# A fused causal convolution and SwiGLU block on one core: cast and transpose of x by transfers instead of by engines

## Chip, cores and metric

The kernel runs on one core of one Trainium2 chip. The metric is device time in microseconds (us), the median of several runs.

## The reference, cut to what matters

```python
# x: 8 x 4096 x 192, weight: 8 heads x 7 taps; w_gate, w_val: 192 x 1536; w_out: 1536 x 192
w = softmax(weight, axis=-1)                       # per head, 24 channels each
x_pad = concatenate([zeros(B, 6, D), x], axis=1)   # six zero rows ahead of each sequence
y[b, s, c] = sum_k w[head(c), k] * x_pad[b, s + k, c]      # seven taps
y = y.reshape(32768, 192)
g = y @ w_gate
out = (g * sigmoid(g) * (y @ w_val)) @ w_out       # float32
```

## The kernel before, in words

The 32768 tokens are cut into 64 blocks of 512 (`TB`), and the blocks go in 32 pairs; a sequence is 4 pairs (`ppb`). The 192 channels of one block are 128 and 64 (`P` and `DB`), so the convolution of a pair is done in three groups of 128 partitions with tokens along the free axis: `A0` and `A1`, the first 128 channels of either block, and `B`, the last 64 of both.

The main loop counts chunks (`at`): a block has 12 (`NCH`), one for 128 of the 1536 hidden columns, a pair has 24. In a chunk `Block.first` multiplies the convolved tokens by the gate and value weights. With 192 = 3 x 64 it uses the two halves of TensorE's rows side by side: gate from partitions 0 to 63 (L344), value from 64 to 127 (L345), three of each. For this each group's result `xc` also exists with its halves swapped, `xs`, which two transfers on SP's queue make (`swap`, L318 and L319). `gate` has ACT write `silu` (L349) and VectorE multiply it by `val` into `h` (L351). `second` multiplies the `h` of the block before by the output weights (L356), four pairs of matmuls a chunk; every sixth chunk ACT copies two finished sub-blocks out (`evacuate`, L394) and SP stores them (`store`, L386). In PSUM, `gate` has two banks, `val` three, `acc` two, and the transposed input `xt` one.

While a pair is multiplied, the next one is convolved. SP fetches x of a pair as float32 with the 128 tokens before it (`emit_fetch`, L73), two pairs ahead; POOL casts it to fp16 in three instructions (`emit_cast`, L210 to L212; L203 to L206 for the first pair, where ACT helps). TensorE transposes each group by matmuls with an identity, 64 x 64 at a time, low and high halves mixed with the matmuls of `second` (`turns`, L265; nine a group), with waits on SP to keep the order inside a bank (`mark`, L222). Of the seven taps ACT copies the transposed group to SBUF (`copy`, L283) and makes three products from that copy (`start_d`, L287, and two `act_tap`, L291); VectorE adds two taps into `aD`, reading the transposed group in PSUM (`dve_tap`, L295); POOL makes two products (`pool_tap`, L302) and adds up (L308, and `join`, L312).

Every engine works off its instructions in the order in which the program issues them. That order is written out by hand: `PLAN["start"]` gives the chunk of the pair in which each group's transposes stand (`first` for pair 1), the other entries how many chunks later each step of the group is issued.

The opening (pair 0) is separate: the transposes of pair 0 are 128 wide (`turn`, L249 and L251), the swapped halves of its first block come from TensorE (L443), group `B` is convolved by TensorE (`sumB`, L424) with matrices that VectorE makes (`diag`, L410), and POOL issues the casting transfers of the weights (L121, L451).

Of the kernel before, what the change touches and what calls it, by code (L numbers as in the profile page):

```python
# [13 lines left out]
    start={"B": 0, "A0": 7, "A1": 15},  # L14
    first={"B": 4, "A0": 10, "A1": 18},
    aP1=(3, 5), taps1=(2, 3), pool1=5, nact1=2, npool1=2,
    copy=1, aD=2, aP=(4, 6), taps=(2, 4), pool=6, fetch=6, fetch1=10, cast=11,
    swap={"B": 13, "A0": 12, "A1": 13}, swap1={"B": 11, "A0": 11, "A1": 11},
    nact=2, npool=2, gate=2, val=3,
# [4 lines left out]
def kernel(  # L24
# [40 lines left out]
    tpool = ctx.enter_context(tc.tile_pool(name="xts", bufs=1, space=bass.MemoryType.PSUM))  # L65
# [3 lines left out]
    def emit_fetch(p, later_than=None):  # L69
        x_sb = xpool.tile([P, 1 + 2 * SUBS, D], fp32, tag="x_sb", name="x_sb", bufs=2)  # L70
        t0 = p * 2 * TB
        lo = 0 if p % ppb else 1
        ins = nc.sync.dma_start(  # L73
            out=x_sb[:, lo:, :],
            in_=x_flat[t0 - P * (1 - lo) : t0 + 2 * TB, :].rearrange("(s p) d -> p s d", p=P),
        )
# [15 lines left out]
    x_sbs = {0: xpool.tile([P, 1 + 2 * SUBS, D], fp32, tag="x_sb", name="x_sb", bufs=2)}  # L92
    halves = [
        nc.sync.dma_start(
            out=x_sbs[0][:, 1 + b * SUBS :, :][:, 0:SUBS, :],
# [4 lines left out]


# [13 lines left out]

    if n_pairs > 1:
        x_sbs[1] = emit_fetch(1, halves[1])

    def load_w(lo, hi, which):
# [24 lines left out]
        for n, shape, dt in (  # L144
            ("xt_act", [P, DB + TB], fp16),
            ("wn_ps", [P, 2, K], fp32),
# [4 lines left out]
            ("idle", [P, TB], fp32),  # L151
        )
# [8 lines left out]
    own = const_pool.tile([H, D + DB], fp32, tag="own", name="own")  # L161
    nc.gpsimd.memset(own, 1.0)
    for m, at in ((own[:, 0:D], 0), (own[:, D:], P)):
        n = m.shape[1]
        nc.gpsimd.affine_select(
            out=m, in_=m, pattern=[[1, n]],
            compare_op=ALU.is_ge, fill=0.0, base=at, channel_multiplier=-grp,
        )
        nc.gpsimd.affine_select(
            out=m, in_=m, pattern=[[-1, n]],  # L170
            compare_op=ALU.is_ge, fill=0.0, base=grp - 1 - at, channel_multiplier=grp,
        )
# [12 lines left out]
    wn = const_pool.tile([P, 2, K], fp32, tag="wn", name="wn")  # L185
    for g in range(2):
# [3 lines left out]
    wsm = {"A": wn[:, 0, :], "B": wn[:, 1, :]}  # L190

    x16s = {}

    def emit_cast(p, first=False):
        x_sb = x_sbs.pop(p)
        xa = xpool.tile([P, 1 + 2 * SUBS, P], fp16, tag="xa", name="xa", bufs=2)
        xb = xpool.tile([P, 1 + SUBS, 2, DB], fp16, tag="xb", name="xb", bufs=2)
        lo = 0 if p % ppb else 1
        if lo:
            nc.gpsimd.memset(xb[:, 0, 0, :], 0.0)  # L200
            nc.gpsimd.memset(xa[:, 0, :], 0.0)
        if first:
            nc.gpsimd.tensor_copy(xa[:, lo : SUBS + 1, :], x_sb[:, lo : SUBS + 1, 0:P])  # L203
            nc.scalar.copy(xb[:, lo:, 0, :], x_sb[:, lo : SUBS + 1, P:D])
            nc.scalar.copy(xb[:, :, 1, :], x_sb[:, SUBS:, P:D])
            nc.gpsimd.tensor_copy(xa[:, SUBS + 1 :, :], x_sb[:, SUBS + 1 :, 0:P])  # L206
            for b in range(2):
                load_w(C1, 2 * C1, b)
        else:
            nc.gpsimd.tensor_copy(xb[:, lo:, 0, :], x_sb[:, lo : SUBS + 1, P:D])  # L210
            nc.gpsimd.tensor_copy(xb[:, :, 1, :], x_sb[:, SUBS:, P:D])
            nc.gpsimd.tensor_copy(xa[:, lo:, :], x_sb[:, lo:, 0:P])  # L212
        x16s[p] = xa, xb


# [10 lines left out]
    def mix(long, short):  # L226

        n = max(len(long), 1)
        for i in range(n):
            if long:  # L230
                long[i]()
            for t in short[i * len(short) // n : (i + 1) * len(short) // n]:
                t()

    class Group:


        def __init__(self, p, g, pool=cpool):
            self.p, self.g, self.w, self.pool = p, g, wsm[g[0]], pool
            self.parts = []  # L240

        def rows(self, s):
            xa, xb = x16s[self.p]
            if self.g == "B":
                return xb[:, s, :, :].rearrange("p b c -> p (b c)")
            return xa[:, s + SUBS * (self.g == "A1"), :]
# [9 lines left out]

        def turns(self):


            self.xt = tpool.tile([P, DB + TB], fp16, tag="xt", name="xt")  # L260
            ends = []

            def one(s, r):
                at = s * P - DB + r
                ins = nc.tensor.transpose(  # L265
                    self.xt[:, at : at + DB], self.rows(s)[r : r + DB, :], ident[r : r + DB, r : r + DB]
                )
                if (s, r) == (0, DB):
                    sync_after(ins, ends[0])
                if (s, r) == (SUBS, 0):  # L270
                    ends.append(mark(ins))

            low = [lambda s=s: one(s, 0) for s in range(1, SUBS + 1)]
            high = [lambda s=s: one(s, DB) for s in range(SUBS + 1)]
            return low, high
# [46 lines left out]
    class Block:  # L322
# [11 lines left out]
        def first(self, j):  # L334
# [72 lines left out]
    nc.vector.tensor_copy(part[0], wsm["B"])  # L407
    nc.vector.tensor_tensor(part[1], wsm["B"], part[0], op=ALU.subtract)
# [31 lines left out]
    for g, ps, copy in (("A0", idle, nc.vector.tensor_copy), ("B", early["swB"], nc.scalar.copy)):  # L440
# [25 lines left out]
    def plan(x):  # L466
        na, npl = PLAN["nact" + x], PLAN["npool" + x]
        ks = [1 + i for i in range(6)]
        acts, dves, pools = ks[:na], ks[na : 6 - npl], ks[6 - npl :]

        def pool_work(g):
            own, g.parts = g.parts, []
            for k in pools:
                g.pool_tap(k)
            for a in own:
                g.parts.append(a)
                g.add()
            g.join()

        steps = [(PLAN["copy"], Group.copy), (PLAN["aD"], lambda g: g.start_d(False))]  # L480
        for k, o in zip(acts, PLAN["aP" + x]):
            steps.append((o, lambda g, k=k: g.act_tap(k, False)))
        for k, o in zip(dves, PLAN["taps" + x]):
            steps.append((o, lambda g, k=k: g.dve_tap(k)))
        return steps + [(PLAN["pool" + x], pool_work)]

    plans = {"": plan(""), "1": plan("1")}

    before = None
    owed, high = [], []  # L490
    todo = {}
    at = 0
    for p in range(n_pairs):
        for bi in range(2):
            block = Block(2 * p + bi)
            for j in range(NCH):
                if at % 24 == PLAN["fetch" if p else "fetch1"] and p + 2 < n_pairs:
                    x_sbs[p + 2] = emit_fetch(p + 2)
# [83 lines left out]
```

## Time and profile before

| what | value |
|---|---|
| median of 3 runs | 789.12 us (788.87 to 789.64) |
| profiled execution: span from first to last instruction | 787.6 us |
| granted TensorE clock, mean | 1.000 |
| from the start to the first `gate` matmul | 15.4 us |
| one pair of the middle, 24 chunks | 23.9 us |
| DMA, mean rate | 88 GB/s |

The profiled execution is one more run, and its time is known by its span; the runs' median is 1.5 us above it. Lines like L345 are lines of the kernel before. PE is TensorE's matmuls, PEld its weight loads, DVE VectorE, ACT ScalarE, POOL GpSimd, SP the engine that issues most transfers (SPq: its queue). Rows of groups give busy time and the mean duration of one instruction; matmuls overlap, so that their rows add up to more than the time they take.

### The profile page before, as it was taken

The numbers are of one execution on the slowest core, as the hardware profiler recorded it, in microseconds if no ns is written. First come the engines' busy times: TensorE is split into PE (matmuls) and PEld (weight loads), VectorE is DVE, ScalarE is ACT, GpSimd is POOL, SyncE is SP. The second block draws the span as 40 slices with busy tenths as digits, with TensorE's granted clock in tenths as the row PEclk, the third lists the DMA queues.
The fourth block names the chain that finished last, engine by engine and source line by source line (L and its number), as shares of the span: only waits on it lengthen the run. The fifth ranks groups of instructions, "written<-read, shape, count | busy, mean of one in ns | idle before, by whom it ended". The sixth has DMA issues, their size and how long they took to land.

```text
span 787.6 us, 29354 instructions
## 1 busy us (share of the span) xinstructions
PE 778.4 (99%) x11635; PEld 695.8 (88%) x11635; DVE 638.3 (81%) x980; ACT 701.0 (89%) x1286; POOL 670.0 (85%) x689
## 2 busy tenths in 40 slices
PE   7999999999999999999999999999999999999998
PEld 3789999999999999999999999999999999999997
DVE  7888888878888888888888888788888888888874
ACT  6999999999899989899999999998999898999974
POOL 7899898888899888898888998888998888988840
PEclk9999999999999999999999999999999999999999
DMA  9333313333223333223333133332233332233111
GB/s 192 80 100 93 91 53 100 97 86 104 78 69 100 92 92 90 69 85 92 103 95 90 55 94 97 91 103 80 62 101 98 90 89 67 85 95 104 48 46 52
DMA packets 89178, 69.07 MB, mean 88 GB/s; under 512 B 7248, under 2 KB 88656, under 8 KB 89040
## 3 DMA queue, kind: packets, MB, share of 16 engines
q1 hardware_dynamic: 86656, 65.82, 29.5%
q0 software_dynamic: 2384, 1.38, 1.2%
q8 instruction: 91, 1.49, 0.8%
q14 instruction: 47, 0.39, 0.2%
HBM read 31.06 MB, written 25.17 MB: 71 GB/s over the span
## 4 chain that ended last, share of the span: by engine, by line
PE 96%; DMA 2%; POOL 1%; SPq 0%; ACT 0%; issue 0%; DVE 0%
PE val L345 35%; PE gate L344 31%; PE acc L356 27%; PE xt L265 2%; DMA x_sb<-in_x_dram 2%; ACT silu L349 0%; SPq L113 0%; POOL xcA L312 0%; POOL t L308 0%; POOL xa L212 0%; PE gate L356 0%; PE val L356 0%; ACT t L291 0%; DVE h L351 0%; SPq L319 0%
## 5 line engine op out<-in xcount | busy, mean ns | idle before, releaser
L351 DVE TENSOR_TENSOR h<-silu,val 128x512 f16<-128x512 f16 x768 | 513.5, 684 | 138.4 <-ACT silu L349 69.2
L349 ACT ACTIVATE silu<-gate 128x512 f16<-128x512 f32 x768 | 449.2, 595 | 70.6 <-PE gate L344 57.6
L356 PE MATMUL acc<-wo_sb,h 64*128 64x192 f16 x6096 | 421.6, 243 | 0.3 <-DVE h L351 0.3
L308 POOL TENSOR_TENSOR t<-t,t 128x512 f32<-128x512 f32 x281 | 357.2, 1271 | 62.6 <-ACT t L291 47.1
L356 PEld LDWEIGHTS <-h 64*128 64x128 f16 x6144 | 372.5, 94 | 25.7 <-DVE h L351 0.5
L344 PE MATMUL gate<-xcA,w_sb 64*128 64x512 f16 x768 | 288.7, 376 | 1.5 <-ACT silu L349 0.8
L345 PE MATMUL val<-xcA,w_sb 64*128 64x512 f16 x768 | 288.8, 376 | 0.4 <-DVE h L351 0.4
L345 PE MATMUL val<-xsA,w_sb 64*128 64x512 f16 x768 | 288.8, 376 | 0.0
L344 PE MATMUL gate<-xsA,w_sb 64*128 64x512 f16 x768 | 288.7, 376 | 0.0
L344 PEld LDWEIGHTS <-w_sb 64*128 64x128 f16 x2304 | 209.2, 94 | 28.1 <-issue 1.1
L345 PEld LDWEIGHTS <-w_sb 64*128 64x128 f16 x2304 | 208.1, 94 | 9.5 <-issue 2.4
L295 DVE SCALAR_TENSOR_TENSOR aD<-xt,wn,aD 128x512 f32<-128x512 f16 x194 | 145.0, 748 | 0.4 <-PE xt L251 0.2
L344 PE MATMUL gate<-xsB,w_sb 64*128 64x512 f16 x384 | 144.4, 376 | 0.0
L345 PE MATMUL val<-xcB,w_sb 64*128 64x512 f16 x384 | 144.4, 376 | 0.0
L345 PE MATMUL val<-xsB,w_sb 64*128 64x512 f16 x384 | 144.4, 376 | 0.0
L344 PE MATMUL gate<-xcB,w_sb 64*128 64x512 f16 x384 | 144.3, 376 | 0.0
L302 POOL TENSOR_SCALAR t<-xcin,wn 128x512 f32<-128x512 f16 x186 | 127.0, 697 | 13.2 <-ACT xcin L283 13.1
L291 ACT ACTIVATE t<-xcin,wn 128x512 f32<-128x512 f16 x188 | 134.2, 714 | 0.0
L312 POOL TENSOR_TENSOR xcA<-t,aD 128x512 f16<-128x512 f32 x63 | 80.0, 1269 | 4.9
L287 ACT ACTIVATE aD<-xcin,wn 128x512 f32<-128x512 f16 x94 | 67.0, 713 | 0.0
L394 ACT COPY o<-acc 128x384 f32<-128x384 f32 x126 | 60.6, 481 | 3.0 <-PE acc L356 0.6
L283 ACT COPY xcin<-xt 128x518 f16<-128x518 f16 x94 | 55.0, 585 | 0.9 <-PE xt L265 0.7
(78 smaller groups left out, 256.7 us busy)
## 6 DMA issues: line engine op xcount, KB each, us to landing
out_dram<-o SPq DMA_DIRECT2D x128, 192.0 KB, 2.0
x_sb<-in_x_dram SPq DMA_DIRECT2D x24, 864.0 KB, 5.2
xsA<-xcA SPq DMA_DIRECT2D x126, 64.0 KB, 2.0
x_sb<-in_x_dram SPq DMA_DIRECT2D x7, 768.0 KB, 4.9
xsB<-xcB SPq DMA_DIRECT2D x62, 64.0 KB, 2.0
x_sb<-in_x_dram SPq DMA_DIRECT2D x2, 384.0 KB, 3.9
wo_sb<-in_moe_w_out_dram POOLq DMA_DIRECT2D x1, 576.0 KB, 7.5
w_st<-in_moe_w_gate_dram SPq DMA_DIRECT2D x1, 384.0 KB, 4.6
```

What stands on the lines that cost most here:

```text
L287: nc.scalar.mul(self.aD, *self.tap(0, psum, xt))
L291: nc.scalar.mul(self.parts[-1], *self.tap(k, psum, xt))
L295: nc.vector.scalar_tensor_tensor(out=self.aD, in0=v, scalar=s, in1=self.aD, op0=ALU.mult, op1=ALU.add)
L302: nc.gpsimd.tensor_scalar(self.parts[-1], v, scalar1=s, scalar2=1.0, op0=ALU.mult, op1=ALU.mult)
L308: nc.gpsimd.tensor_tensor(self.parts[0], self.parts[0], t, op=ALU.add)
L312: (eng or nc.gpsimd).tensor_tensor(xc, self.parts[0], self.aD, op=ALU.add)
L344: nc.tensor.matmul(g, w[0:DB, ca, f], a[0:DB, :], start=(i == 0), stop=(i == 2))
L345: nc.tensor.matmul(v, w[DB:P, cb, f], b[DB:P, :], start=(i == 0), stop=(i == 2))
L349: nc.scalar.activation(s, self.g.pop(j), AF.Silu)
L351: nc.vector.tensor_tensor(h, s, self.v.pop(j), op=ALU.mult)
L356: ins = nc.tensor.matmul(acc, self.h[j][r, ts(s, P)], wo_r[r, j, :], start=first and j == 0, stop=not first and j == NCH - 1, skip_group_c ...
L394: nc.scalar.copy(self.o[:, 2 * half : 2 * half + 2, :], self.acc[:, :, 0:D])
```

## The change

From pair 1 on, a casting transfer issued by POOL (`emit_cast`) copies x from DRAM to a DRAM buffer in fp16, 528 rows of 384: the 16 tokens before and the 512 of a block, with both blocks of the pair side by side. One transposing transfer issued by SP (`emit_turn`) brings it to SBUF as `xt`, 128 x 3 x 528. The 384 columns make three groups of 128: block 0's channels 0 to 127; its last 64 with block 1's first 64; block 1's last 128. `Group` works on `xt` in SBUF in place of `xcin` and PSUM: the transposing matmuls (`turns`), ACT's copy, POOL's casts and the order waits go, and VectorE's taps read SBUF (`dve_tap` with `psum=False`, in the opening for the last group of pair 0 as well). At the head of a sequence POOL zeroes 16 columns (`emit_blank`). The order is given anew, in chunks before the pair's first chunk: cast at -54, transposing transfer at -40, groups from -27, -19 and -11; for pair 1, whose cast and transfer are issued in the opening, groups from chunks 3, 9 and 16. `gate` gets the PSUM bank that becomes free, and the pools of the main loop take over the opening's banks tile by tile (`reuse_waits`).

```diff
 PLAN = dict(
-    start={"B": 0, "A0": 7, "A1": 15},
-    first={"B": 4, "A0": 10, "A1": 18},
-    aP1=(3, 5), taps1=(2, 3), pool1=5, nact1=2, npool1=2,
-    copy=1, aD=2, aP=(4, 6), taps=(2, 4), pool=6, fetch=6, fetch1=10, cast=11,
-    swap={"B": 13, "A0": 12, "A1": 13}, swap1={"B": 11, "A0": 11, "A1": 11},
-    nact=2, npool=2, gate=2, val=3,
+    start=(-27, -19, -11),
+    first=(3, 9, 16),
+    aD=0, aP=(2, 4), taps=(1, 3), pool=4, swap=11,
+    cast=-54, turn=-40,
+    nact=2, npool=2, gate=3, val=3,
 )
...
-    tpool = ctx.enter_context(tc.tile_pool(name="xts", bufs=1, space=bass.MemoryType.PSUM))
+    dpool = ctx.enter_context(tc.tile_pool(name="x16d", bufs=3, space=bass.MemoryType.DRAM))
...
-    def emit_fetch(p, later_than=None):
...
+    HIST = 16
+    ROWS = HIST + TB
+    drams, xts = {}, {}
+
+    def emit_cast(q):
+        t0 = q * 2 * TB - HIST
+        d = dpool.tile([ROWS, 2 * D], fp16, tag="x16d", name="x16d")
+        src = bass.AP(
+            tensor=x_flat.tensor,
+            offset=x_flat[t0 : t0 + 1, :].offset,
+            ap=[[D, ROWS], [TB * D, 2], [1, D]],
+        )
+        nc.gpsimd.dma_start(out=d[:, :].rearrange("r (b c) -> r b c", b=2), in_=src)
+        drams[q] = d
+
+    def emit_turn(q):
+        xt = xpool.tile([P, 3, ROWS], fp16, tag="xt", name="xt", bufs=3)
+        nc.sync.dma_start(out=xt[:, :, :], in_=drams.pop(q)[:, :], transpose=True)
+        xts[q] = xt
+
+    def emit_blank(q):
+        nc.gpsimd.memset(xts[q][:, 0, 0:HIST], 0.0)
+        nc.gpsimd.memset(xts[q][0:DB, 1, 0:HIST], 0.0)
...
-    x_sbs = {0: xpool.tile([P, 1 + 2 * SUBS, D], fp32, tag="x_sb", name="x_sb", bufs=2)}
+    x_sb = xpool.tile([P, 2 * SUBS, D], fp32, tag="x_sb", name="x_sb", bufs=1)
...
-        x_sbs[1] = emit_fetch(1, halves[1])
...
-    def emit_cast(p, first=False):
...
+    x16 = xpool.tile([P, 1 + SUBS, 2, D], fp16, tag="x16", name="x16", bufs=1)
+    nc.gpsimd.memset(x16[:, 0, 0, :], 0.0)
+    nc.gpsimd.tensor_copy(x16[:, 1:, 0, 0:P], x_sb[:, 0:SUBS, 0:P])
+    nc.scalar.copy(x16[:, 1:, 0, P:D], x_sb[:, 0:SUBS, P:D])
+    nc.scalar.copy(x16[:, :, 1, 0:DB], x_sb[:, SUBS - 1 :, 0:DB])
+    nc.gpsimd.tensor_copy(x16[:, :, 1, DB:D], x_sb[:, SUBS - 1 :, DB:D])
+    for b in range(2):
+        load_w(C1, 2 * C1, b)
...
-            self.p, self.g, self.w, self.pool = p, g, wsm[g[0]], pool
+            self.p, self.g, self.w, self.pool = p, g, wn[:, g, :], pool
+            if p:
+                self.xc_in = xts[p][:, g, HIST - pad :]
             self.parts = []
...
-        def turns(self):
...
-            return low, high
...
-        def dve_tap(self, k):
-            v, s = self.tap(k)
+        def dve_tap(self, k, psum=False):
+            v, s = self.tap(k, psum)
...
-            A, B = f"A{self.bi}", "B"
-            xA, sA, xB, sB = xcs[self.p, A], xcs[self.p, A, "S"], xcs[self.p, B], xcs[self.p, B, "S"]
-            lo = ((xA, 0), (sA, 1), (sB if self.bi else xB, 2))
-            hi = ((xA, 1), (sA, 0), (xB if self.bi else sB, 2))
+            a, b = (1, 2) if self.bi else (0, 1)
+            xA, sA, xB, sB = xcs[self.p, a], xcs[self.p, a, "S"], xcs[self.p, b], xcs[self.p, b, "S"]
+            if self.bi:
+                lo = ((sA, 0), (xB, 1), (sB, 2))
+                hi = ((xA, 0), (sB, 1), (xB, 2))
+            else:
+                lo = ((xA, 0), (sA, 1), (xB, 2))
+                hi = ((xA, 1), (sA, 0), (sB, 2))
...
-            A1.turn(tpool.tile([P, DB + TB], fp16, tag="xt", name="xt"))
+            A1.turn(early["xtC"])
...
     if n_pairs > 1:
         emit_cast(1)
+    if n_pairs > 2:
+        emit_cast(2)
     for k in (2, 3, 4, 5):
         A1.dve_tap(k)
     A1.add()
     A1.join()
+    if n_pairs > 1:
+        emit_turn(1)
     A1.swap()
     opening.close()
...
-    gpool = ctx.enter_context(tc.tile_pool(name="gates", bufs=PLAN["gate"], space=bass.MemoryType.PSUM))
-    vpool = ctx.enter_context(tc.tile_pool(name="vals", bufs=PLAN["val"], space=bass.MemoryType.PSUM))
-    apool = ctx.enter_context(tc.tile_pool(name="acc", bufs=1, space=bass.MemoryType.PSUM))
-
-
-
-    def plan(x):
...
-    plans = {"": plan(""), "1": plan("1")}
+    gpool = ctx.enter_context(tc.tile_pool(name="gates", bufs=PLAN["gate"], reuse_waits="tile", space=bass.MemoryType.PSUM))
+    vpool = ctx.enter_context(tc.tile_pool(name="vals", bufs=PLAN["val"], reuse_waits="tile", space=bass.MemoryType.PSUM))
+    apool = ctx.enter_context(tc.tile_pool(name="acc", bufs=1, reuse_waits="tile", space=bass.MemoryType.PSUM))
...
+    todo = {}
+
+    def at_chunk(c, f):
+        todo.setdefault(c, []).append(f)
+
+    ks = list(range(1, K))
+    na, npl = PLAN["nact"], PLAN["npool"]
+    acts, dves, pools = ks[:na], ks[na : len(ks) - npl], ks[len(ks) - npl :]
+
+    def pool_work(g):
...
+    def plan_group(q, g, c):
+        def begin():
+            group = Group(q, g)
+            group.start_d(False)
+            for k, o in zip(acts, PLAN["aP"]):
+                at_chunk(c + o, lambda k=k: group.act_tap(k, False))
+            for k, o in zip(dves, PLAN["taps"]):
+                at_chunk(c + o, lambda k=k: group.dve_tap(k))
+            at_chunk(c + PLAN["pool"], lambda: pool_work(group))
+            at_chunk(c + PLAN["swap"], group.swap)
+
+        at_chunk(c + PLAN["aD"], begin)
+
+    for q in range(1, n_pairs):
+        base = 2 * NCH * q
+        if q > 2:
+            at_chunk(base + PLAN["cast"], lambda q=q: emit_cast(q))
+        if q > 1:
+            at_chunk(base + PLAN["turn"], lambda q=q: emit_turn(q))
+        if q % ppb == 0:
+            at_chunk(base + PLAN["start"][0] - 2, lambda q=q: emit_blank(q))
+        for g in range(3):
+            plan_group(q, g, base + PLAN["start"][g] if q > 1 else PLAN["first"][g])
...
-                if at % 24 == PLAN["fetch" if p else "fetch1"] and p + 2 < n_pairs:
-                    x_sbs[p + 2] = emit_fetch(p + 2)
                 end = before is not None and j % 6 == 5
                 los, his = before.second(4) if before is not None else ([], [])
                 if not end:
                     block.first(j)
-                if high and high[0] <= at:
-                    mix(owed, high[1])
-                    owed, high = [], []
-                if p + 1 < n_pairs:
...
                 for lo, hi in zip(los, his):
                     lo()
                     hi()
-                if before is not None and j % 6 == 5:
+                if end:
                     before.evacuate(j // 6)
-                if end:
                     block.first(j)
                 block.gate(j)
-                if before is not None and j % 6 == 5:
+                if end:
                     before.store(j // 6)
-                for f, gr in todo.pop(at, ()):
-                    f(gr)
+                for f in todo.pop(at, ()):
+                    f()
...
```

More of the change, by code (lines that the diff above doesn't have):

```diff
@@ L64 @@
     opool = ctx.enter_context(tc.tile_pool(name="out", bufs=2))
-    tpool = ctx.enter_context(tc.tile_pool(name="xts", bufs=1, space=bass.MemoryType.PSUM))
+    dpool = ctx.enter_context(tc.tile_pool(name="x16d", bufs=3, space=bass.MemoryType.DRAM))
     ctx.enter_context(tc.manual_schedule())
-    def emit_fetch(p, later_than=None):
[L70 to L75, printed above, removed]
-        )
-        if later_than is not None:
-            sync_after(ins, later_than, "the first pair goes first")
-        return x_sb
+    HIST = 16
[8 more added lines that the diff above has]
+            ap=[[D, ROWS], [TB * D, 2], [1, D]],
+        )
+        nc.gpsimd.dma_start(out=d[:, :].rearrange("r (b c) -> r b c", b=2), in_=src)
[7 more added lines that the diff above has]
+        nc.gpsimd.memset(xts[q][0:DB, 1, 0:HIST], 0.0)
     def sync_after(ins, earlier, why="one bank, two halves of the array"):
@@ L91 @@
     nc.sync.dma_start(out=taps, in_=weight)
-    x_sbs = {0: xpool.tile([P, 1 + 2 * SUBS, D], fp32, tag="x_sb", name="x_sb", bufs=2)}
+    x_sb = xpool.tile([P, 2 * SUBS, D], fp32, tag="x_sb", name="x_sb", bufs=1)
     halves = [
         nc.sync.dma_start(
-            out=x_sbs[0][:, 1 + b * SUBS :, :][:, 0:SUBS, :],
+            out=x_sb[:, b * SUBS : (b + 1) * SUBS, :],
             in_=x_flat[b * TB : (b + 1) * TB, :].rearrange("(s p) d -> p s d", p=P),
@@ L114 @@
         )
-    if n_pairs > 1:
-        x_sbs[1] = emit_fetch(1, halves[1])
     def load_w(lo, hi, which):
@@ L145 @@
             ("xt_act", [P, DB + TB], fp16),
-            ("wn_ps", [P, 2, K], fp32),
+            ("wn_ps", [P, 3, K], fp32),
             ("xtB", [P, DB + TB], fp16),
@@ L151 @@
             ("idle", [P, TB], fp32),
+            ("xtC", [P, DB + TB], fp16),
         )
@@ L158, in warm @@
             nc.tensor.matmul(idle, ident, zeros, start=True, stop=True)
-    own = const_pool.tile([H, D + DB], fp32, tag="own", name="own")
+    own = const_pool.tile([H, 2 * D], fp32, tag="own", name="own")
     nc.gpsimd.memset(own, 1.0)
-    for m, at in ((own[:, 0:D], 0), (own[:, D:], P)):
-        n = m.shape[1]
+    for m in (own[:, 0:D], own[:, D:]):
         nc.gpsimd.affine_select(
-            out=m, in_=m, pattern=[[1, n]],
-            compare_op=ALU.is_ge, fill=0.0, base=at, channel_multiplier=-grp,
+            out=m, in_=m, pattern=[[1, D]],
+            compare_op=ALU.is_ge, fill=0.0, base=0, channel_multiplier=-grp,
         )
         nc.gpsimd.affine_select(
-            out=m, in_=m, pattern=[[-1, n]],
-            compare_op=ALU.is_ge, fill=0.0, base=grp - 1 - at, channel_multiplier=grp,
+            out=m, in_=m, pattern=[[-1, D]],
+            compare_op=ALU.is_ge, fill=0.0, base=grp - 1, channel_multiplier=grp,
         )
@@ L184 @@
     wn_ps = early["wn_ps"]
-    wn = const_pool.tile([P, 2, K], fp32, tag="wn", name="wn")
-    for g in range(2):
+    wn = const_pool.tile([P, 3, K], fp32, tag="wn", name="wn")
+    for g in range(3):
         nc.tensor.matmul(wn_ps[:, g, :], own[:, ts(g, P)], soft, start=True, stop=True)
@@ L189 @@
     nc.vector.tensor_copy(wn, wn_ps)
-    wsm = {"A": wn[:, 0, :], "B": wn[:, 1, :]}
-    x16s = {}
-    def emit_cast(p, first=False):
[L195 to L213, printed above, removed]
+    x16 = xpool.tile([P, 1 + SUBS, 2, D], fp16, tag="x16", name="x16", bufs=1)
[6 more added lines that the diff above has]
+        load_w(C1, 2 * C1, b)
     xcs = {}
@@ L224, in mark @@
         return nop
[L226 to L233, printed above, removed]
     class Group:
         def __init__(self, p, g, pool=cpool):
-            self.p, self.g, self.w, self.pool = p, g, wsm[g[0]], pool
+            self.p, self.g, self.w, self.pool = p, g, wn[:, g, :], pool
+            if p:
+                self.xc_in = xts[p][:, g, HIST - pad :]
             self.parts = []
         def rows(self, s):
[L243 to L246, printed above, removed]
+            return x16[:, s, :, :].rearrange("p b c -> p (b c)")[:, ts(self.g, P)]
         def turn(self, xt, reader=None):
@@ L255, in turn @@
                 self.xt = xt
-        def turns(self):
[L260 to L274, printed above, removed]
-            return low, high
         def tap(self, k, psum=True, xt=None):
@@ L394, in evacuate @@
             nc.scalar.copy(self.o[:, 2 * half : 2 * half + 2, :], self.acc[:, :, 0:D])
-    emit_cast(0, True)
     pool1 = opening.enter_context(tc.tile_pool(name="conv0", bufs=2))
-    A0, GB, A1 = (Group(0, g, pool1) for g in ("A0", "B", "A1"))
+    A0, GB, A1 = (Group(0, g, pool1) for g in range(3))
     A0.turn(early["xt_act"], "act")
@@ L406 @@
     part = [const_pool.tile([P, K], fp16, tag=f"part{i}", name=f"part{i}") for i in range(2)]
-    nc.vector.tensor_copy(part[0], wsm["B"])
-    nc.vector.tensor_tensor(part[1], wsm["B"], part[0], op=ALU.subtract)
+    nc.vector.tensor_copy(part[0], wn[:, 1, :])
+    nc.vector.tensor_tensor(part[1], wn[:, 1, :], part[0], op=ALU.subtract)
     for d, v in zip(diag, part):
@@ L430 @@
     A1.start_d(False)
-    xcB = cpool.tile([P, TB], fp16, tag="xcB", name="xcB")
+    xcB = cpool.tile([P, TB], fp16, tag="xc1", name="xc1")
     nc.scalar.copy(xcB, sumB)
-    xcs[0, "B"] = xcB
+    xcs[0, 1] = xcB
     for k in (2, 3, 4, 5):
-        A0.dve_tap(k)
+        A0.dve_tap(k, True)
     A0.add()
     A0.join(nc.vector)
-    for g, ps, copy in (("A0", idle, nc.vector.tensor_copy), ("B", early["swB"], nc.scalar.copy)):
+    for g, ps, copy in ((0, idle, nc.vector.tensor_copy), (1, early["swB"], nc.scalar.copy)):
         xc = xcs[0, g]
@@ L457 @@
     A1.join()
+    if n_pairs > 1:
+        emit_turn(1)
     A1.swap()
     opening.close()
-    gpool = ctx.enter_context(tc.tile_pool(name="gates", bufs=PLAN["gate"], space=bass.MemoryType.PSUM))
-    vpool = ctx.enter_context(tc.tile_pool(name="vals", bufs=PLAN["val"], space=bass.MemoryType.PSUM))
-    apool = ctx.enter_context(tc.tile_pool(name="acc", bufs=1, space=bass.MemoryType.PSUM))
-    def plan(x):
[L467 to L485, printed above, removed]
@@ new lines @@
+    na, npl = PLAN["nact"], PLAN["npool"]
+    acts, dves, pools = ks[:na], ks[na : len(ks) - npl], ks[len(ks) - npl :]
+    def pool_work(g):
+        own, g.parts = g.parts, []
+        for k in pools:
+            g.pool_tap(k)
+        for a in own:
+            g.parts.append(a)
+            g.add()
+        g.join()
+    def plan_group(q, g, c):
[9 more added lines that the diff above has]
+        at_chunk(c + PLAN["aD"], begin)
@@ L489 @@
+    for q in range(1, n_pairs):
[6 more added lines that the diff above has]
+            at_chunk(base + PLAN["start"][0] - 2, lambda q=q: emit_blank(q))
+        for g in range(3):
+            plan_group(q, g, base + PLAN["start"][g] if q > 1 else PLAN["first"][g])
     before = None
-    owed, high = [], []
-    todo = {}
@@ L502 @@
                     block.first(j)
-                if high and high[0] <= at:
-                    mix(owed, high[1])
-                    owed, high = [], []
-                if p + 1 < n_pairs:
-                    for name, c in PLAN["start" if p else "first"].items():
-                        if at % 24 == c:
-                            gr = Group(p + 1, name)
-                            low, hi_t = gr.turns()
-                            high = (at + 1, hi_t)
-                            mix(his[:2], low)
-                            his, los, owed = his[2:], los[:2], los[2:]
-                            x = "" if p else "1"
-                            swap = PLAN["swap" + x][name]
-                            for o, f in plans[x] + [(swap, Group.swap)]:
-                                todo.setdefault(at + o, []).append((f, gr))
-                            if name == "A0" and p + 2 < n_pairs:
-                                todo.setdefault(at + PLAN["cast"], []).append(
-                                    (lambda g: emit_cast(g.p + 1), gr)
-                                )
                 for lo, hi in zip(los, his):
```

## The prediction

> **What bounds the kernel now.** First the page's busy shares and its chain of work:
>
> ```profile
> PE 778.4 (99%) x11635; PEld 695.8 (88%) x11635; DVE 638.3 (81%) x980; ACT 701.0 (89%) x1286; POOL 670.0 (85%) x689
> ...
> PE 96%; DMA 2%; POOL 1%; SPq 0%; ACT 0%; issue 0%; DVE 0%
> ```
>
> TensorE is busy 99% and is 96% of the chain. A busy PE need not be PE at its peak, so the windows view comes next: one pair in the middle, the last pair, which has no successor to transpose for, then two chunks with transposes and two without; its second answer is for L265 alone.
>
> ```profile
> 397.56:421.46 23.90, 23.90 (x366) 21.70 (x363) 19.64 (x31) 21.75 (x41) 21.17 (x22) 1.00 0.31 89
> 756.03:779.49 23.46, 23.46 (x339) 21.44 (x335) 16.45 (x25) 16.25 (x29) 1.80 (x2) 1.00 0.13 42
> 397.56:399.67 2.11, 2.11 (x40) 1.86 (x37) 1.61 (x3) 1.66 (x4) 2.03 (x2) 1.00 0.29 97
> 399.67:401.62 1.95, 1.95 (x33) 1.79 (x30) 1.22 (x3) 1.86 (x5) 1.53 (x3) 1.00 0.00 0
> ...
> 397.56:399.67 2.11, 0.58 (x9) 0.52 (x9) 1.00 0.29 97
> ```
>
> Columns: PE, PEld, DVE, ACT, POOL busy, granted clock (1.00), DMA share, GB/s. The middle pair takes 23.90 us, the last one 23.46, and the 27 matmuls fewer (366 against 339) are the transposes. So they cost 0.44 us a pair, not the 1.75 us that adding up their overlapping rows of 190 ns would give. The third number to keep is POOL: 21.17 of 23.90 us.
>
> **Removed from the path.** Pairs 1 to 31 lose their 27 transposes. They stood in pairs 0 to 30; in the first half of pair 0 PE isn't the bound (its chunks come 0.65 to 1.8 us apart, set by ACT and VectorE), so I count 30 x 0.44 = **-13.2 us**.
>
> **Removed off the path.** ACT loses three copies a pair (3 x 0.585 = 1.8 us); it is busy 21.75 of 23.90 us behind PE, so this buys margin, no time. POOL loses three casts (L210 to L212: 0.45 + 0.46 + 1.15, 1.92 us from start to start). SP loses six bank-order waits (L222) and the 864 KB fetch. The freed bank makes the gate buffers three instead of two; in the waits view PE waits for silu 0.8 us in total, so that is nothing.
>
> **Added on POOL: the cast's issue.** The nearest rows are POOL's own casting DMAs: 0.63 to 0.84 us with 192 rows each (L121), 1.06 us with 1536 rows (L451). 1056 rows lie between: 0.91 us. POOL thus saves 1.92 - 0.91 = 1.0 us a pair, off the path.
>
> **Added waits on SP and ACT.** SP's transposing transfer waits for the cast; behind it stand the next group's swap and the block stores. ACT's first conv product waits for the transfer, and the silus queue behind it. The cast is issued 14 chunks (13.7 us) before the transfer, and that 13 chunks (12.7 us) before its first use. The cast lands in 7 to 8 us by POOL's DMA rows (6.8, and 7.5 for 576 KB). The transfer, 405 KB, has no row: from below 2.0 us (a 64 KB swap), from above 5.2 us (864 KB fetch); I take 3.9, the row of 384 KB. Both are covered in the steady state. A late one would hold ACT, then PE, by every us over the lead.
>
> **Where there is no lead: the opening.** Pair 1's cast is queued on POOL behind the output weights:
>
> ```profile
> 13.12 1.06 POOL L451 DMA_DIRECT2D wo_sb<-in_moe_w_out_dram  x1
> ...
> 22.99 0.71 ACT L287 ACTIVATE aD<-xcin,wn 128x512 f32<-128x512 f16 x1
> ...
> wo_sb<-in_moe_w_out_dram POOLq DMA_DIRECT2D x1, 576.0 KB, 7.5
> ```
>
> The weights land at 20.6. The queue in front empties up to 3 us earlier without the 768 KB fetch of pair 1, so 17.6 to 20.6; the cast follows with about 2.1 us (in the trace's packets the weights' 384-byte rows went at some 500 a us) and 0.5 to its signal: 20.2 to 23.2; the transfer 3.9: 24.1 to 27.1. I take 25. ACT now asks for it right after four silus. From there to chunk 12 ACT has one product, six silus and two taps (0.6 + 6 x 0.5 + 2 x 0.6 = 4.8), then a VectorE product: some 5.3 us, so chunk 12 starts at 30.3, not 27.07: **+3.2 us** (ends: -1, if the transfer is there by 21; +7, if it takes 8 us).
>
> **Moved: VectorE's taps read SBUF, not PSUM.** Six a pair, 0.75 us each. With `xt` and `aD` both in SBUF they have two inputs there. The trace has such instructions only in its opening, in the timeline and the `x_sb` rows (minimum/median/maximum in ns):
>
> ```profile
> 5.83 2.50 DVE L410 TENSOR_TENSOR diag<-ident,part 128x896 f16<-128x896 f16 x2
> ...
> L203 POOL CAST xa<-x_sb x1: 612/612/612, 4.9 to 4.9; 128x512 f16<-128x512 f32 x1
> L206 POOL CAST xa<-x_sb x1: 1322/1322/1322, 6.1 to 6.1; 128x512 f16<-128x512 f32 x1
> ...
> 11.41 0.63 POOL L121 DMA_DIRECT2D w_sb<-in_moe_w_val_dram  x1
> ...
> 11.71 2.03 DVE L312 TENSOR_TENSOR xcA<-t,aD 128x512 f16<-128x512 f32 x1
> ...
> 12.03 1.16 POOL L450 CAST w_sb<-w_st 128x1152 f16<-128x1152 f32 x1
> ```
>
> The same POOL cast takes 0.61 us alone and 1.32 beside VectorE's L410; VectorE's L312 takes 2.03, ending 0.55 after POOL's cast: the two take turns. The Trainium skill (SBUF — State Buffer, Who interferes with whom) has the rule: a VectorE instruction with two SBUF inputs and a GpSimd instruction that reads SBUF exclude each other, and whichever starts second is blocked to the end of the first. By that rule L206 agrees; L312 does not, since it began 0.3 us before L450 and yet came last. By the rule a tap waits for one POOL instruction at most, which bounds the port rival below at 800 us; by L312's row it can wait for two or three, its 841.
>
> Two costs follow. First, POOL's time: a group is 6.70 us from start to start without its wait (timeline, 408.37 to 415.32 less 0.24); three are 20.1, the cast's issue 0.9, and each tap that cuts in delays POOL by about 0.75 - 0.36 = 0.39 (L206 ended 0.47 after L410's first half, 0.14 less than its own 0.61, and the next one lost 0.14 too; POOL's gap of 0.08 between adds is used as well): 6 x 0.39 = 2.3. Sum 23.3 of 23.46: full, but not over. Second, a tap delays the h behind it:
>
> ```profile
> 409.41 0.68 DVE L351 TENSOR_TENSOR h<-silu,val 128x512 f16<-128x512 f16 x1
> ...
> 410.66 0.38 PE L345 MATMUL val<-xcA,w_sb 64*128 64x512 f16 x1
> ```
>
> This h follows a tap; three chunks later PE wants its bank, 0.57 us after h ended. After most taps this margin is about 0.6. A tap that waits less costs nothing; above it, PE stalls. In the new order a group's taps come 2.85 and 4.8 us after its first chunk; POOL, held by the last ACT tap, begins a group at 0.7, so its first add runs from 2.1 to 3.4 and its second from 3.9 to 5.2: waits of 0.4 and 0.2 after the overlap. Only the groups behind the cast's issue slip by 0.9 and can meet a full add (1.1 us, 0.5 lost). I take 0.1 us a pair: **+3.1 us** (ends: 0, and 2.1 a pair, below).
>
> **Sum.** The span is 787.6; the median of the runs is 789.1, 1.5 above it, which stays. 789.1 - 13.2 + 3.2 + 3.1 = **782.2**, say 782.
>
> **The rivals.** *Everything is covered*: the transfer arrives by 21 us, no tap waits over its margin: 789.1 - 13.2 = 775.9. For it: each wait computed above is under 0.6. Against: pair 1's cast has no lead. *The port decides (slower)*: POOL is nearly full, so the phases drift and taps land at random. Landing in an add or join of 1.27 us, a tap loses what it waits over 0.6: 4 x 0.67² / 2 / 7.82 = 0.115 us each, 0.69 a pair, 21 in all: 789.1 - 13.2 + 3.2 + 21.4 = 800.5. If POOL also keeps the port across join and the two products behind it (no gap there, 2.63 us; L312 lost to two POOL instructions in a row), (2.03² + 3 x 0.67²) / 2 / 7.82 = 0.35 a tap, 2.1 a pair, 841 at the end. It decides from (13.2 - 3.2) / 31 = 0.32 us a pair on. For it: POOL's 23.3 of 23.46. Against: a PE stall moves the taps back relative to POOL, which settles the phases. *The transfer is later than its lead*: the lead is 14 us (12.7, and 1.3 until ACT comes to it); a miss by 2 us in every pair is 31 x 2 on top: 844. At the casting queue's 63 ns a packet (page: 2384 packets, 1.2% of 16 engines' span) 16 us of all 16 take some 4000 packets, pieces of 100 bytes; no row tells the pieces. The Trainium skill (VectorE: DVE Perf Modes, The three transpose paths) gives 1309 ns for a 128x128 transpose by DMA against 390 on TensorE; 12.4 such tiles one after the other would be an estimated 16.2 us. No run here shows it. *The terms cancel*: stalls of 0.3 a pair leave 789.
>
> **Chances.** Forecast 0.38 (its own range 778 to 787), all covered 0.16, cancelled 0.06, port 0.32, late transfer 0.08. A measurement of this kernel tells about 0.2% (1.6 us) from no change: faster 0.54, same 0.06, slower 0.40. The range goes from 776 (0.04 below it) to 805 (leaving the late transfer and the worse quarter of the port case, 0.16).
>
> **What would show it.** In the profile after: middle pairs near 23.5 us with 339 PE matmuls; VectorE's tap rows at 0.75 to 1.3 us mean instead of 0.75; POOL adds no longer all 1.27; ACT's first product of pair 1 waiting for a DMA until about 25 us; chunk 12 at 30. I am wrong if PE waits for h line after line (port), if ACT waits for `xt` in every pair (transfer), or if pairs without transposes still take 23.9.

## The result, and the profile after

The changed kernel takes 812.23 us (median of 4 runs, 812.05 to 813.06) against 789.15 for the kernel before: 1.029 times its time [1.0276, 1.0305], slower by 23 us where 7 less were forecast. The profiled execution spans 811.3 us, 23.7 more than before. First the page's busy shares, its granted clock in 40 slices and its chain of work:

```profile
PE 777.9 (96%) x10800; PEld 588.4 (73%) x10800; DVE 653.0 (80%) x980; ACT 660.4 (81%) x1193; POOL 713.9 (88%) x626
...
PEclk9799999999999999999999999999999999999999
...
PE 80%; POOL 8%; issue 5%; DVE 3%; ACT 2%; DMA 2%; ACTq 0%; POOLq 0%; DVEq 0%
```

PE has 835 instructions fewer (10800, 11635 before), yet TensorE is 80% of the chain instead of 96%, and POOL's share has risen from 1 to 8%. Something on POOL is now waited for. The windows view says where, one row for each kind of pair: pair 0, pair 3, pair 7, pair 8, pair 9 (columns: time, then PE, PEld, DVE, ACT, POOL busy, granted clock, DMA share, GB/s):

```profile
15.55:47.58 32.03, 24.79 (x242) 13.78 (x243) 23.14 (x33) 20.75 (x38) 23.78 (x21) 0.84 0.71 97
95.67:125.70 30.03, 26.21 (x340) 17.20 (x338) 20.75 (x31) 22.02 (x40) 24.38 (x26) 0.89 0.39 68
197.17:222.77 25.60, 23.99 (x339) 17.96 (x337) 20.57 (x31) 21.77 (x40) 22.10 (x24) 1.00 0.38 80
222.77:246.23 23.46, 23.46 (x339) 18.24 (x337) 19.56 (x31) 20.43 (x38) 22.50 (x20) 1.00 0.47 87
246.23:270.24 24.01, 23.64 (x339) 18.20 (x337) 20.21 (x31) 20.43 (x38) 23.05 (x21) 1.00 0.42 85
```

From pair 4 on the pattern repeats every four pairs, the length of a sequence: 23.46, 24.01, 24.01, 25.60. Pair 8 is what the prediction expected of all of them: 339 matmuls in 23.46 us. The other three kinds carry the loss. Of the 23.7 us in the span, the transposes give -13.2 (30 x 0.44, as forecast). Pair 0 adds 8.5 (32.03 against 23.54) and pair 1 some 1.0 (24.57 against 24.06 - 0.44). The seven pairs in which the head of the next sequence is convolved add 6.6 once and 2.14 six times, 19.4 together. Fourteen pairs at 24.01 add 0.55 each, 7.7. That makes 23.4; the other 0.3 lies in small differences.

The waits view names the waits that were hardly there before, when the largest wait of PE's val for h was 0.4 us (engine, line, waited for: total us, times, longest):

```profile
ACT aD L246 <- POOL xt L90: 15.5, 7, 4.7
...
PE val L308 <- DVE h L314: 12.3, 24, 1.9
...
POOL t L261 <- DMA xt<-x16d: 6.7, 1, 6.7
ACT aD L246 <- DMA xt<-x16d: 5.8, 1, 5.8
```

The last two are the opening, once. The first is L90, the second of `emit_blank`'s two instructions, which zero the 16 columns ahead of a sequence: seven times ACT's first product (L246) waits for it. The timeline around the second of these, at pair 7's first chunk (197.17), shows how (start, duration, engine, line; in brackets the idle time before and its releaser):

```profile
194.85 1.27 POOL L271 TENSOR_TENSOR xc<-t,aD 128x512 f16<-128x512 f32 x1
...
196.06 1.27 POOL L80 DMA_DIRECT2D x16d<-in_x_dram  x1
...
196.89 0.57 POOL L89 MEMSET xt<- 128x16 f16 x1
196.93 0.58 POOL L90 MEMSET xt<- 64x16 f16 x1
...
197.49 0.72 ACT L246 ACTIVATE aD<-xt,wn 128x512 f32<-128x512 f16 x1 [1.81 <-POOL xt L90]
...
198.12 0.58 ACT L312 ACTIVATE silu<-gate 128x512 f16<-128x512 f32 x1
...
198.73 0.69 DVE L314 TENSOR_TENSOR h<-silu,val 128x512 f16<-128x512 f16 x1 [2.33 <-ACT silu L312]
```

The rows of the two zeroings read 0.6 us together, most of it beside the end of the cast's issue (196.06 + 1.27 = 197.33). In the program they stand behind all of the previous group's work on POOL (`pool_work`, issued two chunks earlier, 6.7 us of it) and behind the cast's issue (one chunk earlier). POOL is done with them at 197.5, ACT has then been idle for 1.81 us, its silus stand in line behind the product, and VectorE's h comes late for TensorE, after 2.33 us in which VectorE was idle.

In the 24.01 us pairs it is the port, the access to SBUF that VectorE's taps and POOL share (`e4` below tests it). The timeline of pair 9, POOL's and VectorE's rows:

```profile
246.00 2.34 POOL L261 TENSOR_SCALAR t<-xt,wn 128x512 f32<-128x512 f16 x2
...
246.47 0.75 DVE L254 SCALAR_TENSOR_TENSOR aD<-xt,wn,aD 128x512 f32<-128x512 f16 x1
...
248.43 4.29 POOL L267 TENSOR_TENSOR t<-t,t 128x512 f32<-128x512 f32 x3
...
248.76 1.48 DVE L254 SCALAR_TENSOR_TENSOR aD<-xt,wn,aD 128x512 f32<-128x512 f16 x1
```

The second tap begins 0.33 us after POOL's first add and takes 1.48 us instead of 0.75: the 0.5 us kind of loss that the prediction worked out. Three adds take 4.29 us instead of 3.8 (3 x 1.27). In the whole run the groups and the transfers read (busy and mean ns; KB and median us to landing):

```profile
L267 POOL TENSOR_TENSOR t<-t,t 128x512 f32<-128x512 f32 x281 | 406.7, 1447 | 46.4 <-ACT t L250 21.8 <-DVE aD L254 4.8
...
L254 DVE SCALAR_TENSOR_TENSOR aD<-xt,wn,aD 128x512 f32<-128x512 f16 x190 | 165.1, 869 | 0.5 <-PE xt L230 0.4
...
x16d<-in_x_dram POOLq DMA_DIRECT2D x31, 396.0 KB, 6.4
...
xt<-x16d SPq DMA_TRANSPOSE x31, 4.0
```

The transfers behave as priced: the transposing one lands after a median of 4.0 us (3.9 forecast), the cast after 6.4 (7 to 8 forecast). In the opening they have no lead, as SP's and ACT's timelines show:

```profile
23.14 1.77 SPq L85 DMA_TRANSPOSE xt<-x16d  x1
```

```profile
21.33 0.60 ACT L312 ACTIVATE silu<-gate 128x512 f16<-128x512 f32 x1 [2.40 <-PE gate L307]
27.69 0.72 ACT L246 ACTIVATE aD<-xt,wn 128x512 f32<-128x512 f16 x1 [5.76 <-DMA xt<-x16d]
```

SP issues the transfer for pair 1 at 23.14, and ACT, done with its silus, stands still for 5.76 us until 27.69.

### The profile page after: what moved, and what is told of

Its sections match the earlier page's. It is cut to its first block, busy times and chain, and to the rows that moved or that the text cites. A ratio compares the mean times of both kernels' runs of the same rounds, so it can differ in the third digit from the quotient of the medians.

```text
span 811.3 us, 27341 instructions
## 1 busy us (share of the span) xinstructions
PE 777.9 (96%) x10800; PEld 588.4 (73%) x10800; DVE 653.0 (80%) x980; ACT 660.4 (81%) x1193; POOL 713.9 (88%) x626
## 4 chain that ended last, share of the span: by engine, by line
PE 80%; POOL 8%; issue 5%; DVE 3%; ACT 2%; DMA 2%; ACTq 0%; POOLq 0%; DVEq 0%
PE val L308 40%; PE acc L319 28%; PE gate L307 11%; POOL t L267 3%; DVE h L314 2%; POOL xc L271 2%; ACT silu L312 1%; POOL x16d L80 1%; DVE aD L254 1%; DMA x16d<-in_x_dram 1%; POOL t L261 1%; DMA xt<-x16d 1%; ACT t L250 0%; PE idle L165 0%; POOL w_sb L410 0%
## 5 line engine op out<-in xcount | busy, mean ns | idle before, releaser
L319 PE MATMUL acc<-wo_sb,h 64*128 64x192 f16 x6096 | 469.0, 243 | 9.7 <-ACT o L357 9.5
L267 POOL TENSOR_TENSOR t<-t,t 128x512 f32<-128x512 f32 x281 | 406.7, 1447 | 46.4 <-ACT t L250 21.8
L308 PE MATMUL val<-xc,w_sb 64*128 64x512 f16 x1152 | 425.1, 378 | 12.4 <-DVE h L314 12.3
L307 PE MATMUL gate<-xc,w_sb 64*128 64x512 f16 x1152 | 430.5, 379 | 4.4 <-ACT silu L312 4.4
L307 PE MATMUL gate<-xs,w_sb 64*128 64x512 f16 x1152 | 430.3, 378 | 0.0
L308 PE MATMUL val<-xs,w_sb 64*128 64x512 f16 x1152 | 375.1, 379 | 0.5 <-DMA xs<-xc 0.5
L261 POOL TENSOR_SCALAR t<-xt,wn 128x512 f32<-128x512 f16 x186 | 148.1, 893 | 7.1 <-DMA xt<-x16d 6.7
L250 ACT ACTIVATE t<-xt,wn 128x512 f32<-128x512 f16 x186 | 133.0, 715 | 0.0
L271 POOL TENSOR_TENSOR xc<-t,aD 128x512 f16<-128x512 f32 x94 | 121.4, 1291 | 8.0 <-DVE aD L254 0.7
L246 ACT ACTIVATE aD<-xt,wn 128x512 f32<-128x512 f16 x93 | 66.4, 714 | 21.3 <-POOL xt L90 15.5
L90 POOL MEMSET xt<- 64x16 f16 x7 | 4.0, 576 | 0.0
```

The source lines that it names most:

```text
L246: nc.scalar.mul(self.aD, *self.tap(0, psum, xt))
L250: nc.scalar.mul(self.parts[-1], *self.tap(k, psum, xt))
L261: nc.gpsimd.tensor_scalar(self.parts[-1], v, scalar1=s, scalar2=1.0, op0=ALU.mult, op1=ALU.mult)
L267: nc.gpsimd.tensor_tensor(self.parts[0], self.parts[0], t, op=ALU.add)
L271: (eng or nc.gpsimd).tensor_tensor(xc, self.parts[0], self.aD, op=ALU.add)
L307: nc.tensor.matmul(g, w[0:DB, ca, f], a[0:DB, :], start=(i == 0), stop=(i == 2))
```

## The experiments

Theory: the slowdown is two things put in the wrong place, the zeroing in POOL's order and pair 1's cast in the opening. Rival: the port that VectorE's taps and POOL share, whose cost the wait for the zeroing only reflects, since POOL is late because taps hold it up. Beside the first four runs below the kernel before measured 789.24 us, beside the other four 789.34.

**Zeroing on VectorE** (`e1_blank_vector`). The same columns are zeroed by another engine:

```diff
 def emit_blank(q):
-    nc.gpsimd.memset(xts[q][:, 0, 0:HIST], 0.0)
-    nc.gpsimd.memset(xts[q][0:DB, 1, 0:HIST], 0.0)
+    nc.vector.memset(xts[q][:, 0, 0:HIST], 0.0)
+    nc.vector.memset(xts[q][0:DB, 1, 0:HIST], 0.0)
```

> The 16 columns at the head of a sequence are zeroed by VectorE instead of POOL, at the same chunk. Theory (three separate places; this one is the order: ACT's first product waits for a zeroing that stands on POOL behind a whole group's adds and a cast): ACT waits no more for xt L90, the head pairs fall from 25.6 (the first from 30.0) to 23.5 to 24.0 us, and the time from 812.2 by 19.4 to 793; up to 802 if, without the stall that sets POOL back in step every fourth pair, all pairs show the 24.0 us that now only two in four show. Rival (POOL is overloaded by the port, and the zeroing is only where that shows): ACT or PE wait elsewhere instead, over 806.

Measured 788.61 us, 0.9992 [0.9982, 1.0001] of before: 23.6 less than the changed kernel, and below the 793 that was expected. The waits view has no wait for L90 left. A pair in the middle of the windows view, then the taps and adds:

```profile
214.64:238.10 23.46, 23.46 (x339) 18.19 (x337) 19.72 (x31) 20.43 (x38) 22.50 (x20) 1.00 0.45 87
```

```profile
L267 POOL TENSOR_TENSOR t<-t,t 128x512 f32<-128x512 f32 x281 | 393.9, 1402 | 24.7 <-ACT t L250 2.3
...
L254 DVE SCALAR_TENSOR_TENSOR aD<-xt,wn,aD 128x512 f32<-128x512 f16 x190 | 153.6, 809 | 0.6 <-PE xt L230 0.5
```

The port is still fought over (taps 809 ns, adds 1402), but all pairs from 2 to 29 take 23.46 to 23.49 us. The 24.01 us pairs went together with the stalls at the heads, so they need the stall; that it shifts the taps against POOL's adds, every four pairs anew, is argued from the timelines.

**Cast earlier in the opening** (`e3_cast_earlier`). Pair 1's cast is queued ahead of the middle part of the weights instead of behind the output weights:

```diff
+    emit_cast(1)
     for b in range(2):
         load_w(C1, 2 * C1, b)
 ...
-    if n_pairs > 1:
-        emit_cast(1)
```

> Only pair 1's cast is issued earlier, on POOL ahead of the weights' casting transfers; its transposing transfer stays where it is. Theory (no lead in the opening): the transfer lands by about 18 us instead of 27.7, ACT's first product of pair 1 waits no more, the clock stays at 1.0, chunk 12 starts near 27 instead of 35: 803 to 805, with pairs from the third on as they were. Rival (the opening is long because POOL and VectorE have too much in it, or because of the clock itself): chunk 12 after 32, over 808.

Measured 804.67 us, 1.0195 [1.018, 1.0211]. Pair 0 in the windows view:

```profile
15.07:40.10 25.03, 21.28 (x242) 13.17 (x243) 23.34 (x33) 20.87 (x38) 22.88 (x21) 1.00 0.77 112
```

25.03 instead of 32.03, at clock 1.00, and chunk 12 at 27.2 us. The later pairs keep their pattern, and L90 is still waited for, 14.0 us in seven waits. Pair 3 falls from 30.03 to 28.13 us; otherwise the opening and the heads are separate losses.

**The sum in PSUM** (`e4_sum_in_psum`). From pair 1 on ACT writes `aD` to PSUM, so that a tap has one input there; its last tap writes an SBUF tile, which POOL reads. `gate` gives up its third bank for it:

```diff
-    nact=2, npool=2, gate=3, val=3,
+    nact=2, npool=2, gate=2, val=3,
 ...
-            self.aD = self.pool.tile([P, TB], fp32, tag="aD", name="aD")
+            self.aD = (aps[0] if self.p else self.pool).tile([P, TB], fp32, tag="aD", name="aD")
 ...
+            out = self.aD
+            if self.p and k == 4:
+                out = self.pool.tile([P, TB], fp32, tag="aDs", name="aDs")
 ...
+    aps.append(ctx.enter_context(tc.tile_pool(name="ads", bufs=1, reuse_waits="tile", space=bass.MemoryType.PSUM)))
```

> ACT writes its first product of each group into a PSUM bank (taken from gate, two instead of three), and VectorE's taps read the sum from there, so that each tap has one SBUF input; the second one writes SBUF for POOL's join. Theory (the shared port): all taps at 0.75 us, POOL's adds back at 1.27, the pairs of 24.01 at 23.46: 804.5, some us less if the zeroing on POOL comes earlier too. Rival (the 0.55 us come from the cast's issue on POOL, not from the port): pairs stay at 24.0, 811 to 813.

Measured 793.03 us, 1.0048 [1.003, 1.0066], more of a gain than expected. Its groups, then its waits:

```profile
L272 POOL TENSOR_TENSOR t<-t,t 128x512 f32<-128x512 f32 x281 | 356.6, 1269 | 92.9 <-ACT t L251 58.4 <-DVE aDs L258 18.6 <-DVE h L319 1.2
...
L258 DVE SCALAR_TENSOR_TENSOR aD<-xt,wn,aD 128x512 f32<-128x512 f16 x97 | 72.7, 749 | 0.3 <-PE xt L231 0.2
```

```profile
ACT aD L247 <- POOL xt L90: 8.1, 7, 1.2
```

Taps are back at 749 ns and adds at 1269: the two engines no longer meet. The Trainium skill (SBUF — State Buffer, Who interferes with whom) says that a VectorE instruction with at most one SBUF input, outside VectorE's 2-port modes, does not contend with GpSimd; these two rows agree. The wait for the zeroing remains at 1.2 us a head, which costs 0.93 (head pairs of 24.39), and there are no 24.01 us pairs. So either edit alone removes those: they need a stall and a shared port. The heads shrink as well, though the zeroing stands where it stood: seven at 0.93 are 6.5 us where the changed kernel lost 19.4. With the 7.7 of the other pairs, 20.6 us go from pairs 2 to 30; pair 1 gives 2.8 back, as TensorE waits 2.03 us there for a swap. So the rival holds in part: most of a head's loss needs the port too, because POOL comes later to the zeroing when taps hold up its adds. (The edit also takes a bank from `gate`; it is the rows of taps and adds that tie the gain to the port.)

**All three** (`e5_all_three`).

> The three edits together. Theory: 31 pairs of 23.46 us and the opening of before, 789.1 - 13.2 + 1 = 777. If the three places share one cause and give the loss on to each other: 785 and over.

Measured 780.33 us, 0.9885 [0.987, 0.99], 3.3 more than expected. The pairs from 2 on are 23.5; pair 1 takes 27.63. The waits view has a new line, and the timelines of SP, of POOL and of PE show where it comes from:

```profile
PE val L314 <- DMA xs<-xc: 2.5, 1, 2.5
```

```profile
36.28 0.59 SPq L284 DMA_DIRECT2D xs<-xc  x1
```

```profile
33.49 1.29 POOL L80 DMA_DIRECT2D x16d<-in_x_dram  x1
```

```profile
38.74 0.38 PE L313 MATMUL gate<-xc,w_sb 64*128 64x512 f16 x1
41.63 0.58 PE L314 MATMUL val<-xs,w_sb 64*128 64x512 f16 x1 [2.51 <-DMA xs<-xc]
```

The second half of a swap, issued at 36.28, is there at 41.6, 5.3 us later where the median of these transfers is 2.9. The cast of pair 3, issued 2.8 us ahead of it, has its packets on the DMA engines from 35.5 to 40.9; that they hold up the swap is argued from this overlap. Pair 1's groups stand 21, 15 and 8 chunks ahead of its first chunk, those of later pairs 27, 19 and 11, so that here the delay reached TensorE.

**Zeroing earlier, on POOL** (`e2_blank_earlier`). The zeroing stays on POOL but is issued ahead of the previous group's work:

```diff
-    at_chunk(base + PLAN["start"][0] - 2, lambda q=q: emit_blank(q))
+    at_chunk(base - 33, lambda q=q: emit_blank(q))
```

> The zeroing stays on POOL, but is issued four chunks earlier, ahead of the last group's adds of the pair before and of the cast. Theory (the place in POOL's order is the cause, not POOL's load): no wait of ACT for xt L90, all pairs from the third on at 23.5, 787 to 790, as with VectorE's zeroing. Rival (whatever stands on POOL is late): some of the 1.7 to 2.1 us a head stays, 793 or more.

Measured 788.99 us, 1.0002 [0.9982, 1.0022]: the same as with the zeroing on VectorE. Four chunks of place in a queue are worth 23 us; POOL has as much work as in the changed kernel. The zeroings themselves are short there, as rows of its groups show:

```profile
L89 POOL MEMSET xt<- 128x16 f16 x7 | 0.8, 115 | 0.0
L90 POOL MEMSET xt<- 64x16 f16 x7 | 0.7, 104 | 0.0
```

**Two without PSUM** (`e7_two_no_psum`). The edits of `e1` and `e3` together; the taps keep both inputs in SBUF.

> Zeroing on VectorE and the earlier cast, with the taps reading SBUF as in the changed kernel. If the port costs nothing once the zeroing no longer stops ACT: the 780.3 of all three edits, within 1. If it still costs: some 0.1 to 0.5 us a pair more, 783 to 795.

Measured 780.85 us, 0.9906 [0.9877, 0.9935], half a microsecond from all three, though taps take 0.82 us and adds 1.40.

**All three, and pair 1's swaps earlier** (`e6_three_and_swap`). On top of `e5`:

```diff
-    at_chunk(c + PLAN["swap"], group.swap)
+    at_chunk(c + (PLAN["swap"] if q > 1 else 9), group.swap)
```

> All three edits, and for pair 1 the transfers that swap halves are issued two chunks earlier, ahead of a store on SP and of the packets of the fourth pair's cast. With all three edits pair 1 still began with a stall of 3.5 to 4 us, the swapped half of its second group landing behind that cast. Theory: that stall goes, 776 to 777. Rival (POOL's adds are too late for chunk 24 in any order): 780.

Measured 777.81 us, 0.9858 [0.9839, 0.9877], the fastest of all. Its page (span, busy shares, chain):

```profile
span 775.5 us, 27410 instructions
...
PE 765.0 (99%) x10800; PEld 584.0 (75%) x10800; DVE 632.4 (82%) x994; ACT 661.0 (85%) x1193; POOL 648.3 (84%) x612
...
PE 96%; DVE 1%; DMA 1%; ACT 1%; POOL 0%; issue 0%; SPq 0%; POOLq 0%
```

TensorE is 96% of the chain again, with the transposes gone. Pair 1 fell from 27.63 to 24.87 us, all others are 23.46 to 23.50 but for pair 0 (23.98).

**Two and the swaps** (`e8_two_and_swap`). The same without PSUM, to price the port where nothing else stands in the way.

> The earlier swap with the zeroing on VectorE and the earlier cast, taps in SBUF. By the theory 776 to 778, the port costing nothing; by a port that costs 0.1 us a pair or more, 780 and over.

Measured 780.96 us, 0.9892 [0.9877, 0.9907], 3.2 us behind `e6`. The spans differ by 3.8: pairs 0 and 1 take 1.04 and 1.05 more, chunk 0 starts 0.74 later, the last convolved pair takes 0.6 more, and the 28 pairs between 0.4 together. The 0.74 lies ahead of any tap that the edit moves (the first one begins at 22), so it is not the port's. One line of its waits view tells of taps that still met an add:

```profile
PE val L309 <- DVE h L315: 4.1, 7, 1.7
```

The pairs' time hides what the port takes from POOL. From 121 to 730 us POOL has no wait left in the waits views of `e1`, `e2` and `e8`; in `e6` it waits 59.9 us there:

```profile
POOL t L273 <- ACT t L252: 42.4, 55, 1.0
POOL t L273 <- DVE aDs L259: 17.5, 26, 0.9
```

With the taps in SBUF and the stalls gone, POOL just keeps up with TensorE and has no slack for anything that comes on top.

## Why the prediction was wrong, by its own steps

**Removed from the path, -13.2: right.** A middle pair without stalls takes 23.46 us, measured in seven pairs of the changed kernel and in nearly all of `e1`, `e6` and `e7`.

**Added waits on SP and ACT: the step that failed.** It listed what ACT's first product waits for and named the transfer alone. At the head of a sequence the product waits for the zeroing too, an instruction of the diff that the prediction never placed in POOL's order, though it counted POOL as nearly full (23.3 of 23.46 us). The wait is 1.8 us and more because a whole group's work and the cast's issue are queued ahead of it. It cost 19.4 us at the heads and set off the 7.7 in between. `e1` and `e2`, which change nothing but this, bring 23.6 and 23.2 us back, and so show that the loss needs it: work and transfers are the same, only the engine or the place differs. It is not the whole cause. `e4` leaves the zeroing where it was, frees the port and brings 19.2 back; the two gains overlap, and without the port the misplaced zeroing costs 6.5.

**The opening: right in kind, mis-sized.** Chunk 12 starts 8.0 us later than before (35.05 against 27.07) where 3.2 were forecast and 7 was the late end; pair 0 takes 8.5 more. The weights in front of the cast landed at 20.95, no earlier than before (20.6), and the cast by 23.1, at the late end of the bound (20.2 to 23.2); the transfer took 4.5 us from its issue, not 3.9. ACT had it at 27.69, past the 27.1 that was the late end. From there to chunk 12 came 7.4 us, not 5.3: the granted clock was 0.50 from 20.1 to 23.5 and from 26.9 to 33.7, which the prediction did not consider, and ACT waited 1.7 us for gates in that stretch. `e3` returns 7.0 of pair 0 with the clock at 1.0 throughout. In `e7` both fixes give 780.85, near the 782 that was forecast, but by another sum: the opening costs less than forecast there, and pair 1 more.

**Taps and the port: the mechanism right, the size missed in the changed kernel, and met by luck without the stalls.** Forecast were 3.1 us, 0.1 in every pair, with 21 for the port rival. `e8` against `e6` gives 3.2, but the 28 pairs from 2 to 29 have 0.4 of it together; the rest lies in the opening and at the end, and 0.74 is not the port's. The phases do settle, which was the argument against the rival. What the prediction did not see is that a stall from elsewhere unsettles them: in the changed kernel 20.6 us of pairs 2 to 30 go with the port, by `e4`, about the 21 of the rival, though by a stall at each head and not by taps that land at random. No tap in the changed kernel took over 1.87 us, 1.1 more than its own 0.75: it waits for less than one add of 1.27, never for two, so the 841 us case (844 with the opening's 3.2, which its sum leaves out) is out. The rule for the wait in the Trainium skill (the page cited with `e4`) agrees.

**The cast's issue: 1.27 us, not 0.91.** It matters only as 0.36 us more ahead of the zeroing. **The late transfer: refuted.** A median of 4.0 us and at most 5.3 in 31 transfers leave most of the lead unused. From the time that the Trainium skill (VectorE: DVE Perf Modes, The three transpose paths) gives for one 128x128 tile, 16.2 us were estimated for tiles that go one after the other; the measured 4.0 us show that one large transfer does not pay that price per tile.

In part open is why the wait at the first head is the longest: it is 4.7 us and the pair loses 6.6, of which the clock of 0.50 for 6.8 us behind it can account for 3.4 at most. POOL came late from the opening: after the transfer's arrival at 27.7 its waits view shows no wait until this head. The port kept it late: in `e4`, where pair 0 takes as long (31.96 us), POOL waits for others again from 60 us on, and the first head waits 1.16 us like the other six, though its longer pair 1 also gave POOL time. In `e3`, with 7.0 us less in the opening, the same pair still waits 3.2 and loses 4.7, of which 1.7 at most is the clock. How the excess divides between opening and port is not shown.

## What to carry to other kernels

Write down, for each engine that works in program order, every instruction that an edit adds, the small conditional ones too, and what stands ahead of each in its queue: seven zeroings, 0.1 us each where nothing is in their way, cost more here (19.4 us, with the port) than the transposes of 30 pairs had (13.2). Moving work from a bound TensorE to transfers pays here (777.8 against 789.3) once every consumer has its lead, and the lead has to be found separately for the opening and for the heads, not only for the steady state. A stall that recurs can raise the price of an unrelated contention, so judge the contention again when the stall is gone.

## What the runs showed of the hardware that was not expected

**The clock can give way after short pauses.** In `e5` PE has a gap of 2.5 us and the granted clock is 0.50 for 3.4 us (41.3 to 44.7); in the changed kernel it is 0.50 for 6.8 us after the first head, where PE's gap is 3.8. The length alone does not decide: a gap of 2.5 us in `e1` (48.5 to 51.0) was not followed by it, and of two gaps of 1.69 us in the opening the one in `e7` was (0.50 from 20.2 to 23.6) and the one in `e8` was not. The Trainium skill (TensorE: Matmul & The Clock Gate, Part 1) tells of windows of some 3.4 us, one idle window for half the rate; the lengths of 3.4 and 6.8 agree, and gaps shorter than such a window were enough here.

**A short instruction behind a DMA issue reads long on POOL.** In the changed kernel each zeroing reads 0.57 us, 0.4 of it beside the issue of the cast; in `e2`, with no issue just ahead of it, 0.12 and 0.10. On VectorE it takes 65 ns, as a row of `e1`'s groups shows:

```profile
L89 DVE MEMSET xt<- 128x8 uint32 x7 | 0.5, 65 | 0.0
```

So it is short on either engine, and its place in the queue is what cost.
